# Seven block products in the first half of the gMLP input (z1), and a reordered gating

## The chip, the cores and the metric

One core of a Trainium2 chip runs the whole kernel. The metric is the device time of one execution in microseconds; the median of three runs stands for the kernel. The profile is of one further execution, and gives a start and a duration for every instruction on TensorE (PE, with its weight loads as PEld), VectorE (DVE), ScalarE (ACT), GpSimd (POOL) and for the DMAs issued from SyncE (SP) and ACT.

## The reference

A transformer layer in bf16 with 2048 tokens and a width of 1024: a memory attention block, then a gMLP block. The change touches the second one alone:

```python
def _B_ref(x, w_in, w_sp, b_sp, w_out):
    B, S, D = x.shape                     # S = 2048, D = 1024
    F = w_in.shape[-1]                    # 3584
    Fh = F // 2                           # 1792
    z = _gelu(jnp.einsum('bsd,df->bsf', x, w_in))
    z1 = z[..., :Fh].copy()
    z2 = _layernorm(z[..., Fh:], axis=-1)
    g = jnp.einsum('ts,bsf->btf', w_sp, z2) + b_sp[None, :, None]
    return jnp.einsum('bsf,fd->bsd', z1 * g, w_out)
...
h2 = h + _B_ref(_layernorm(h, axis=-1), B_w_in, B_w_sp, B_b_sp, B_w_out)
```

So there are four large products: the z2 half of the input (2048 x 1024 by 1024 x 1792), the z1 half (the same size), the gating (2048 x 2048 by 2048 x 1792), and the output (2048 x 1792 by 1792 x 1024).

## The kernel before, in words

The program is written with a recorder (`_Recorder`, line 34): each call such as `pe.matmul` or `dve.tensor_tensor` is noted on its engine's list in program order, the waits are worked out from the memory cells and PSUM banks that it reads and writes, and every engine then runs its own list in order. Hence nearly all instructions carry line 210. What sets the order on an engine is the order of the calls; a call that must wait holds everything behind it on its engine, SP's DMA queue included. SBUF is one arena in which tensors are placed by hand (`tens`, with an offset in KB); a new tensor at an old place waits for the last reader of the old one.

After the attention, the gMLP has these stages:

- **z2** (`z2_group`, line 798, and the loop from line 931): 64 groups of 8 matmuls, one for each of 16 token tiles and four chunks of 448 columns. The weights are loaded by `win_load`. ACT takes each bank through a gelu into `Z2`, DVE computes its statistics (`z2_stats`), Pool the reciprocal deviations `ZRS`, and `z2_apply` normalizes a token tile into f16 (`Z2H`). The same loop reads the gating matrix row by row (`sp_norm_load` from SP, into two buffers `SJ`) and sums its squares on ACT (`sp_norm`), from which `sp_scale` makes a power of two `SC` and its inverse `INV`, to keep f16 in range. Eight PSUM banks are used in turn (`next_bank`).
- **z1** (lines 1073 to 1104): four token segments of 512 by 14 feature chunks of 128. Each is 8 matmuls over the width (`mm8`), with a weight chunk of `WIZ` (bf16) against `HNT[s]`, the transposed normalized tokens, and ACT takes the bank through the gelu into `Z1T`. Beside it, DVE does the rest of `z2_apply` and prepares the gating's operands: `sp_load` reads blocks of the gating matrix by transposing DMAs, `sp_half` scales a block to f16, `sp_sum` makes T1, T2, T3 and `s_sum` the sums of Z2 blocks (`SS`).
- **gating** (`gate_group`, line 1001): twice (for tokens 0 to 1023 and for 1024 to 2047) seven groups. A group makes a 2 x 2 block of outputs, 1024 tokens by two feature chunks, with seven block products of 8 matmuls in place of eight (Winograd's form of Strassen's scheme). The seven pair A11, A12, A22 and four sums of the Z2 blocks with B11, B21, B22 and T1 to T4 of the gating matrix. DVE adds products that are shared, with the scale and the bias, and multiplies by `Z1T` in place; ACT copies the first product out, and Pool adds the two bias rows to it.
- **output** (`out_unit`): 16 units of 14 matmuls after each gating half, added to what the attention block left in DRAM. The blocks for the second half of the gating are loaded and prepared beside the first 16 units.

In the gating the order of the products over the engines is written out by hand in `gate_group`: each addition on DVE that reads a bank must be done before TensorE adds the next product to the same bank.

Of the kernel before, what the change touches and what calls it, by code (L numbers as in the profile page):

```python
# [5 lines left out]
BF16 = mybir.dt.bfloat16  # L6
# [252 lines left out]
def bass_sequential_preLN__memory_aug_infini_attn__mixer_gmlp__prompt_kernel(  # L259
# [31 lines left out]
    class Bump:  # L291
# [4 lines left out]
        def __call__(self, name, shape, dt):  # L296
# [63 lines left out]
    WIN = [tens("win%d" % i, [128, 8, 512], BF16, o * K) for i, o in enumerate((46, 54, 190))]  # L360
    WIZ = [tens("wiz%d" % i, [128, 8, w], BF16, o * K)
           for i, (o, w) in enumerate(((54, 512), (190, 512), (118, 512), (126, 256)))]
# [3 lines left out]
    ROLES = (("b11", 46), ("b12", 22), ("b21", 198), ("b22", 14))  # L366
    RAW = {k: tens(k + "r", [128, 8, L], BF16, o * K) for k, o in ROLES}
    BH = {k: tens(k + "h", [128, 8, L], F16, o * K)
          for k, o in ROLES + (("t1", 30), ("t2", 190), ("t3", 22), ("t4", 38))}
    SS = tens("ss", [128, 4, 8, 128], F16, 54 * K)  # L370
# [3 lines left out]
    ZRS = b3("zrs", [128, NTC], F32)  # L374
    ONES = b3("ones", [128, 128], BF16)
    MHZ = b3("mhz", [128, 1], F32)
    SQ = b3("sq", [128, 16], F32)
    SQB = b3("sqb", [128, 16], BF16)
    TOT = b3("tot", [128, 1], F32)
    TOP = b3("top", [128, 1], F32)  # L380
    SC = b3("sc", [128, 1], F32)
    INV = b3("inv", [128, 1], F32)
# [3 lines left out]
    BROW = [tens("brow%d" % i, [128, L], BF16, (132 + i) * K) for i in range(2)]  # L386
    WO0 = tens("w_out0", [128, 14, 512], BF16, 118 * K)
    WO1A = tens("w_out1a", [128, 7, 512], BF16, 54 * K)
    WO1B = tens("w_out1b", [128, 7, 512], BF16, 4 * K)
    FIN = [tens("fin%d" % i, [128, 512], BF16, o * K) for i, o in enumerate((61, 11, 12, 13))]  # L390
# [399 lines left out]
    CH = [("z2", FH + 448 * k, 448) for k in range(4)] + [("z1", 512 * k, min(512, FH - 512 * k)) for k in range(4)]  # L790

    def win_load(k):
        kind, lo, w = CH[k]
        sp.dma_start((WIN[k % 3] if k < 4 else WIZ[k - 4])[:, :, 0:w], wcols(B_w_in, lo, lo + w))

    zs, zq, staged = [], [], []

    def z2_group(k, tc, stage=None):
        s, tcl = divmod(tc, 4)
        b = next_bank()  # L800
        wi = WIN[k % 3]
        mm8(PS[:, b, 0:448], lambda i: HNT[s][:, i, tcl * 128:(tcl + 1) * 128], lambda i: wi[:, i, 0:448])
        if stage is None:
            z2_gelu(k, tc, PS[:, b, 0:448])
        else:
            act.activation(ZSTG[stage][:], PS[:, b, 0:448], ACTF.Copy)
            staged.append((k, tc, ZSTG[stage][:]))
# [5 lines left out]
    def z2_stats():  # L813
        k, tc = zs.pop(0)
        dve.bn_stats(ZST[:, tc, k, :], Z2[:, tc, k * 448:(k + 1) * 448])
        if k == 3:
            dve.bn_aggr(ZMV[:, tc, :], ZST[:, tc, :, :])
            pool.tensor_single_scalar(ZRS[:, tc:tc + 1], ZMV[:, tc, 1:2], float(LN_EPS), ALU.add)
            pool.tensor_tensor(ZRS[:, tc:tc + 1], ZRS[:, tc:tc + 1], MHALF[:], ALU.pow)
            zq.append(tc)  # L820

    def z2_apply():
        tc = zq.pop(0)
        dve.tensor_scalar(Z2H[:, tc, :], Z2[:, tc, :], ZMV[:, tc, 0:1], ZRS[:, tc:tc + 1], ALU.subtract, ALU.mult)

# [93 lines left out]
    def sp_scale(b):  # L919
        pe.matmul(PS[:, b, 0:16], ONES[:], SQB[:], start=True, stop=True)  # L920
        dve.tensor_reduce(out=TOT[:], in_=PS[:, b, 0:16], axis=mybir.AxisListType.X, op=ALU.add)
        dve.tensor_single_scalar(TOT[:], TOT[:], 1e-30, ALU.max)
        pool.tensor_tensor(TOP[:], TOT[:], MHZ[:], ALU.pow)
        dve.tensor_single_scalar(TOP[:].bitcast(I32), TOP[:].bitcast(I32), 0x7F800000, ALU.bitwise_and)
        dve.tensor_single_scalar(SC[:], TOP[:], 8192.0, ALU.mult)
        dve.reciprocal(INV[:], SC[:])

# [3 lines left out]
    for it in todo:  # L931
# [9 lines left out]
        if it[0] and it[1] > 3 or it[0] > 1:  # L941
            q = 16 * it[0] + it[1] - 20
            r = (q * 16 + 15) // 44
            if r < 16 and (q * 16 - 1) // 44 < r:
                sp_norm(r)
                if r < 14:
                    sp_norm_load(r + 2)
                elif r == 15:
                    pool.tensor_copy(SQB[:], SQ[:])
# [4 lines left out]
        if len(zq) > 1:  # L954
            z2_apply()
        if it == (0, NTC - 1):
            win_load(3)
        if it == (1, NTC - 1):
            for k in (4, 6, 7):
                win_load(k)  # L960
        if it == (2, NTC - 1):
            win_load(5)
# [8 lines left out]
    def sp_half(k):  # L971
        dve.tensor_single_scalar(BH[k][:], RAW[k][:], SC[:], ALU.mult)

    def sp_sum(o, a, b):
        dve.tensor_tensor(BH[o][:], BH[a][:], BH[b][:], ALU.subtract)
# [20 lines left out]
    def prod1(g):  # L996
        b = next_bank()
        prod(b, a_blk(0, 0, g), "b11", True)
        return b

    def gate_group(pr, g, ba):
        t1, t2 = slice(1024 * pr, 1024 * pr + 512), slice(1024 * pr + 512, 1024 * pr + 1024)
        s1, s1b1, s1b2, u2, u3 = (TMP[k][:] for k in ("s1", "s1b1", "s1b2", "u2", "u3"))
        inv = INV[:]

        def stt(o, b, add):
            dve.scalar_tensor_tensor(o, bank(b), inv, add, ALU.mult, ALU.add)

        def out(v, i, t):
# [3 lines left out]
        act.activation(s1, bank(ba), ACTF.Copy, scale=inv)  # L1013
        pool.tensor_tensor(s1b2, s1, BROW[1][:], ALU.add)
        pool.tensor_tensor(s1b1, s1, BROW[0][:], ALU.add)
        bb, bc = next_bank(), next_bank()
        prod(bb, SS[:, 1], "t2", True)
        prod(bc, SS[:, 0], "t1", True)
        stt(u2, bb, s1b2)
        if pr == 0 and g == 0:  # L1020
            sp_sum("t4", "b21", "t2")
        if g < 6:
            s_sum(1, g + 1)
        prod(bb, SS[:, 2], "t3", False)
        prod(ba, a_blk(0, 1, g), "b21", False)
        stt(u3, bb, s1b2)
        stt(u3, bc, u3)
        out(u3, 1, t2)
        nb = prod1(g + 1) if g < 6 else None
        if g < 6:  # L1030
            s_sum(3, g + 1)
        stt(s1, ba, BROW[0][:])
        out(s1, 0, t1)
        prod(bc, SS[:, 3], "b22", False)
        if g < 6:
            s_sum(2, g + 1)
        prod(bb, a_blk(1, 1, g), "t4", False)
        stt(u2, bc, u2)
        out(u2, 0, t2)
        if g < 6:  # L1040
            s_sum(4, g + 1)
        stt(s1b1, bb, s1b1)
        out(s1b1, 1, t1)
        return nb
# [24 lines left out]
    for j in range(4):  # L1069
        sp_load(0, "b21", j)  # L1070
    for j in range(4):
        sp_load(0, "b11", j)
    for s in range(NSEG):
        for fc in range(14):
            k, fl = divmod(fc, 4)
            b = next_bank()
            mm8(bank(b), lambda i: WIZ[k][:, i, fl * 128:(fl + 1) * 128], lambda i: HNT[s][:, i, :])
            act.activation(Z1T[:, fc, s * 512:(s + 1) * 512], bank(b), ACTF.Gelu_apprx_tanh)
            if zq:
                z2_apply()  # L1080
            if s == 0 and fc == 6:
                sp_scale(next_bank())
            if s == 2 and fc in (6, 12):
                for k in ("b21", "b11", "b22") if fc == 6 else ("b12",):
                    sp_half(k)
            if s == 3:
                if fc == 0:
                    sp_sum("t1", "b12", "b11")
                if fc == 4:
                    s_sum(1, 0)  # L1090
                    s_sum(2, 0)
                    s_sum(3, 0)
                    s_sum(4, 0)
                if fc == 2:
                    sp_sum("t3", "b22", "b12")
                if fc == 8:
                    sp_sum("t2", "b22", "t1")
        if s == 0:
            for j in range(4):
                sp_load(0, "b22", j)  # L1100
        if s == 1:
# [82 lines left out]
```

## Time and profile before

| | |
|---|---|
| median of 3 runs | 772.08 us (772.01 to 772.38) |
| the profiled execution | 772.03 us |
| its span in the profile | 770.3 us |
| TensorE busy | 761.2 us (99%), 5476 matmuls |
| DVE, ACT, POOL busy | 464.5, 334.2, 200.0 us |
| z2 from its last attention part to z1 | 338.3 to 404.6 us |
| z1 | 404.6 to 501.3 us |
| first gating half, output units, second gating half | 501.3, 586.0, 634.4 us to 719.2 us |
| a matmul of 512 columns, in a row of them | recorded with 379 ns, the next one starts some 216 ns later |

How to read it: the page's span is the time from the first to the last instruction. Matmuls are pipelined, so the duration of one is longer than the distance to the next, and their ends are modelled; the pace is read from a stretch of time and the number of matmuls that were issued in it. (A few per cent of the matmul records can be missing.) In a timeline line the columns are the start, the duration, the engine, the operation with output and inputs, the shapes, the count, and in brackets the idle time before it with what ended it. A group's line ends in its busy time, the mean of one in ns, and the idle time before it.

### The profile page before, as it was taken

What the parts mean: (1) busy time and instruction counts of PE and PEld (TensorE: products, weight loads), DVE (VectorE), ACT (ScalarE), POOL (GpSimd) and SP (SyncE); (2) the same over time, 40 slices, a digit from 0 to 9 for tenths busy, and PEclk for the clock granted to TensorE, in tenths of its full rate; (3) what the DMA queues carried; (4) which work ended last, traced back from release to release, by engine and by line L of the source; (5) the groups of instructions that cost most, each with busy time, mean ns of one, the idle gap of its engine ahead of it and who ended that gap; (6) DMA issues with size and microseconds to landing.
All of it is one profiled execution on the core that took longest, in us unless ns stands there. A gap on an engine that the chain in (4) does not pass through costs nothing.

```text
span 770.3 us, 13128 instructions
## 1 busy us (share of the span) xinstructions
PE 761.2 (99%) x5476; PEld 367.2 (48%) x5551; DVE 464.5 (60%) x846; ACT 334.2 (43%) x395; POOL 200.0 (26%) x361
## 2 busy tenths in 40 slices
PE   8999999999999999999999999999999999999998
PEld 4445555545554545455554444444444444444444
DVE  5586589768964676754366202278785756878422
ACT  6777877777777767157783333310000000000000
POOL 2564556555653333100033000021110002112000
PEclk9999999999999999999999999999999999999999
DMA  9654555364425331765672230020019850000222
GB/s 305 168 152 89 97 83 125 83 97 84 96 57 131 84 83 37 210 173 183 198 219 55 55 67 2 1 96 1 1 34 206 229 169 7 1 1 0 62 83 75
DMA packets 133900, 75.06 MB, mean 97 GB/s; under 512 B 96208, under 2 KB 124624, under 8 KB 133840
## 3 DMA queue, kind: packets, MB, share of 16 engines
q1 hardware_dynamic: 126592, 67.40, 36.0%
q10 hardware_dynamic: 7248, 6.82, 2.8%
q8 instruction: 43, 0.70, 0.4%
q14 instruction: 17, 0.14, 0.1%
HBM read 42.74 MB, written 8.39 MB: 66 GB/s over the span
## 4 chain that ended last, share of the span: by engine, by line
PE 93%; DVE 5%; issue 1%; DMA 1%; ACT 0%; DVEq 0%
PE ps L210 93%; DVE stats L210 1%; DMA wv<-in_A_wv_dram 1%; DVE hch L210 1%; DVE otok L210 0%; DVE pqk L210 0%; DVE lno L210 0%; DVE ta L210 0%; DVE etmp L210 0%; DVE rd L210 0%; DVE rdm L210 0%; DVE mv L210 0%; ACT e L210 0%; ACT L210 0%; DVE upd L210 0%
## 5 line engine op out<-in xcount | busy, mean ns | idle before, releaser
L210 ACT ACTIVATE e<-ps 128x2048 bf16<-128x2048 f32 (+1 forms) x96 | 152.7, 1590 | 41.7 <-PE ps L210 41.5
L210 POOL TENSOR_SCALAR_AFFINE_SELECT e<-e 128x512 bf16<-128x512 bf16 x128 | 90.6, 720 | 132.4 <-ACT e L210 132.3
L210 POOL TENSOR_TENSOR tmp_s1b<-tmp_s,brow 128x512 f32<-128x512 f32 x28 | 32.3, 1155 | 255.1 <-ACT tmp_s L210 223.7
L210 PE MATMUL ps<-win,hnT 128*128 128x448 bf16 x512 | 98.3, 352 | 0.0
L210 PE MATMUL ps<-hnT,wiz 128*128 128x512 bf16 x439 | 96.2, 379 | 0.5
L210 ACT ACTIVATE tmp_s<-ps,inv 128x512 f32<-128x512 f32 x14 | 9.6, 687 | 195.1 <-DVE z1T L210 131.6
L210 PEld LDWEIGHTS ps<-win,hnT 128*128 128x128 bf16 x512 | 49.7, 98 | 46.4 <-issue 0.2
L210 PEld LDWEIGHTS ps<-hnT,wiz 128*128 128x128 bf16 x448 | 43.7, 98 | 52.7
L210 ACT ACTIVATE z1T<-ps 128x512 bf16<-128x512 f32 x56 | 33.4, 597 | 63.3 <-PE ps L210 61.1
L210 PE MATMUL ps<-xnT,wk 128*128 128x512 bf16 x233 | 59.6, 380 | 1.2
L210 PE MATMUL ps<-wv,xnT 128*128 128x512 bf16 x255 | 59.5, 380 | 0.9 <-DMA wv<-in_A_wv_dram 0.5
L210 PE MATMUL ps<-wo,oT 128*128 128x512 bf16 x254 | 57.7, 380 | 0.1
L210 DVE BATCH_NORM_STATS2 zst<-z 128x6 f32<-128x448 bf16 x64 | 38.4, 617 | 31.8 <-ACT z L210 31.3
L210 DVE TENSOR_TENSOR fin<-fin,ps 128x512 bf16<-128x512 bf16 (+2 forms) x33 | 22.1, 671 | 56.6 <-PE ps L210 48.4
L210 PE MATMUL ps<-xnT,wq 128*128 128x512 bf16 x226 | 54.0, 379 | 1.6
L210 PE MATMUL ps<-w_out,z1T 128*128 128x512 bf16 x218 | 49.3, 379 | 0.3
L210 ACT ACTIVATE z<-ps 128x448 bf16<-128x448 f32 x60 | 31.5, 541 | 37.4 <-PE ps L210 37.4
L210 PEld LDWEIGHTS ps<-v,e 128*128 128x128 bf16 x1280 | 38.8, 96 | 14.0 <-issue 6.5
L210 PE MATMUL ps<-v,e 128*128 128x33 bf16 x1280 | 42.2, 178 | 0.0
L210 DVE SCALAR_TENSOR_TENSOR tmp_u<-ps,inv,tmp_s1b 128x512 f32<-128x512 f32 x28 | 21.0, 750 | 31.3 <-PE ps L210 16.7
L210 PEld LDWEIGHTS ps<-wo,oT 128*128 128x128 bf16 x256 | 24.1, 98 | 27.6
L210 PEld LDWEIGHTS ps<-xnT,wk 128*128 128x128 bf16 x256 | 22.6, 98 | 29.9 <-issue 5.0
(137 smaller groups left out, 1101.0 us busy)
## 6 DMA issues: line engine op xcount, KB each, us to landing
sj<-in_B_w_sp_dram SPq DMA_DIRECT2D x16, 512.0 KB, 3.5
xch<-in_A_x_dram SPq DMA_DIRECT2D x16, 256.0 KB, 3.6
xr<-in_A_x_dram SPq DMA_DIRECT2D x16, 256.0 KB, 4.0
out_dram<-hch SPq DMA_DIRECT2D x16, 256.0 KB, 2.4
win<-in_B_w_in_dram SPq DMA_DIRECT2D x4, 896.0 KB, 5.3
wiz<-in_B_w_in_dram SPq DMA_DIRECT2D x3, 1024.0 KB, 6.2
wo<-in_A_wo_dram SPq DMA_DIRECT2D x1, 2048.0 KB, 8.7
fin<-out_dram ACTq DMA_DIRECT2D x16, 128.0 KB, 3.4
```

The source lines that it names most:

```text
L210: ins = getattr(e, op.name)(*op.args, **op.kw)
```

## The change

It has four parts.

1. **z1 by seven block products.** The width is cut into two halves j, the tokens of a pair p of segments into two halves k, and the feature chunks into fc and fc + 7. A group g (14 of them: p = 0 or 1, fc = 0 to 6) makes four output chunks from seven products of 4 matmuls each. They pair four weight blocks and four sums `SZ` of weight blocks (Pool, `sz_sum`) with four token blocks `hb` and four differences `HT` of token blocks (DVE, `hn_sum`; product 5 and 6 use SZ1 and SZ2, 7 uses SZ3, 3 uses SZ4). The weights are now f16 (`WZH`), scaled by a power of two: `wz_norm` takes the largest absolute value of each part, `scale_of` makes scale and inverse, `wz_half` scales. All this happens in the z2 stage, from a list `aux` by step of its loop (step 0 is group (1, 4)). In a z1 group, ACT copies product 1 out of its bank (s1), DVE adds s1 to product 6 (u2) before product 7 is added to the same bank, then u3 = bank + s1 and u3 += product 5, later s1 += bank after product 4 and u2 += bank after product 3; ACT runs the gelu, with the inverse scale, on the four results. The products of all groups are issued in the order of 7 g + `offs`, so that in steady state TensorE does 6, 5, 1 of the next group, 7, 2, 3 of the group before, 4.
2. **What runs beside z1.** No `z2_apply` is left in the z2 stage: 16 of them run in groups 0 to 7, half on DVE, half on ACT (with a small Pool operation before it). The squares of the gating matrix are done by step 35 instead of 41. The scale of the gating is computed in group 1. B11, B12 and B22 are scaled by ACT in quarters (`sp_part`) in groups 8, 9 and 11, B21 by DVE after z1 (`seam`); T1 to T3 are made by DVE in quarters in groups 10 to 13, and T4 in the first gating group (`mid`). Their loads move into z1, B21's to its end.
3. **Gating.** The same seven products, in another order: three first products before the first group, and the second product of group g + 1 within group g; the banks are fixed (0 to 2 for the first product, 3 and 4, 5 and 6 for the others) instead of taken in turn.
4. **Places.** Weights, blocks, `SS`, `BROW`, `FIN` and the output weights lie elsewhere; there is a fourth `WIN` buffer.

The diff, cut to its core:

```diff
+    WZS = ((46, 256), (118, 256), (126, 256), (54, 128))
+    WZ = [tens("wz%d" % i, [128, 8, 2, w], BF16, o * K) for i, (o, w) in enumerate(WZS)]
+    WZH = [tens("wzh%d" % i, [128, 8, 2, w], F16, o * K) for i, (o, w) in enumerate(WZS)]
-    ROLES = (("b11", 46), ("b12", 22), ("b21", 198), ("b22", 14))
+    ROLES = (("b11", 14), ("b12", 22), ("b22", 46), ("b21", 126))
...
+    def scale_of(k, n, b):
+        b = next_bank() if b is None else b
+        pe.matmul(PS[:, b, 0:n], ONES[:], SQB[:, 0:n], start=True, stop=True)
+        dve.tensor_reduce(out=TOT[:], in_=PS[:, b, 0:n], axis=mybir.AxisListType.X, op=ALU.add)
         dve.tensor_single_scalar(TOT[:], TOT[:], 1e-30, ALU.max)
+        if k:
+            dve.reciprocal(TOP[:], TOT[:])
+        else:
+            pool.tensor_tensor(TOP[:], TOT[:], MHZ[:], ALU.pow)
         dve.tensor_single_scalar(TOP[:].bitcast(I32), TOP[:].bitcast(I32), 0x7F800000, ALU.bitwise_and)
+        dve.tensor_single_scalar(SC[k][:], TOP[:], 8192.0, ALU.mult)
+        dve.reciprocal(INV[k][:], SC[k][:])
...
+    def wz_norm(q, r):
+        v = WZ[q][:, 2 * r:2 * r + 2, :, :] if q < 3 else WZ[q][:, 4 * r:4 * r + 4, :, :]
+        dve.tensor_reduce(out=SQZ[:, 4 * q + r:4 * q + r + 1], in_=v.rearrange("p c i w -> p (c i w)"), axis=mybir.AxisListType.X, op=ALU.max,
+                          apply_absolute_value=True)
...
+    def hn_sum(p, t, h, eng=dve):
+        a, b = {1: (hb(0, 1, p), hb(0, 0, p)), 2: (hb(1, 1, p), HT[p][1][:]),
+                3: (hb(1, 1, p), hb(0, 1, p)), 4: (hb(1, 0, p), HT[p][2][:])}[t]
+        s = slice(2 * h, 2 * h + 2)
+        eng.tensor_tensor(HT[p][t][:, s, :], a[:, s, :], b[:, s, :], ALU.subtract)
...
+    def sz_sum(g, k):
+        fc = g % 7
+        a, b, op = {1: (wz_blk(1, 0, fc), wz_blk(1, 1, fc), ALU.add), 2: (sz(g, 1), wz_blk(0, 0, fc), ALU.subtract),
+                    3: (wz_blk(0, 0, fc), wz_blk(1, 0, fc), ALU.subtract),
+                    4: (wz_blk(0, 1, fc), sz(g, 2), ALU.subtract)}[k]
+        pool.tensor_tensor(sz(g, k), a, b, op)
...
+    for r in range(16):
+        q = (37 * r + 15) // 16
+        at(q, sp_norm, r)
+        if r < 14:
+            at(q, sp_norm_load, r + 2)
+    at(37, pool.tensor_copy, SQB[:], SQ[:])
+    for k in range(12):
+        at(k + 1, wz_norm, (1, 2, 0)[k // 4], k % 4)
+    for k in range(8):
+        at(3 + 2 * k, hn_sum, 0, (1, 2, 3, 4)[k // 2], k % 2)
+    at(18, wz_norm, 3, 0)
+    at(19, wz_norm, 3, 1)
+    at(20, pool.tensor_copy, SQB[:, 0:14], SQZ[:])
+    at(25, scale_of, 1, 14, None)
+    for k in range(8):
+        at(26 + k, wz_half, k // 2, k % 2)
+    for k in (1, 2, 3, 4):
+        at(35 + k, sz_sum, 0, k)
...
         if it == (0, NTC - 1):
+            for k in (1, 2, 0):
+                wz_load(k)
             win_load(3)
...
-            mm8(bank(b), lambda i: WIZ[k][:, i, fl * 128:(fl + 1) * 128], lambda i: HNT[s][:, i, :])
-            act.activation(Z1T[:, fc, s * 512:(s + 1) * 512], bank(b), ACTF.Gelu_apprx_tanh)
+        for i in range(4):
+            pe.matmul(b, ka[:, i, :], kb[:, i, :], start=(first and i == 0), stop=(i == 3), skip_group_check=True)
+        if k == 1:
+            act.activation(s1, b, ACTF.Copy)
+        if k == 6:
+            dve.tensor_tensor(u2, b, s1, ALU.add)
+        if k == 5 and g < 13:
+            for x in (1, 2):
+                sz_sum(g + 1, x)
+        if k == 7:
+            dve.tensor_tensor(u3, b, s1, ALU.add)
+            dve.tensor_tensor(u3, bank(zb[g, 2]), u3, ALU.add)
+            z1_out(fc + 7, 2 * p + 1, u3)
+            if g < 13:
+                sz_sum(g + 1, 3)
+        if k == 2:
+            z1_out(fc, 2 * p, b)
+            if g == 0:
+                sz_sum(1, 4)
+        if k == 4:
+            dve.tensor_tensor(s1, b, s1, ALU.add)
+            z1_out(fc + 7, 2 * p, s1)
+        if k == 3:
+            dve.tensor_tensor(u2, b, u2, ALU.add)
+            z1_out(fc, 2 * p + 1, u2)
+            if g < 12:
+                sz_sum(g + 2, 4)
+        for f, a in todo1.get((g, k), ()):
+            f(*a)
...
+    for g in range(8):
+        on(g, 6, lambda: zq and z2_apply())
+        on(g, 4, lambda: zq and z2_apply(True))
+    for k in range(8):
+        on((0, 1, 2, 3, 4, 4, 5, 5)[k], 3 if k < 5 else (7, 3, 7)[k - 5], hn_sum, 1, (1, 2, 3, 4)[k // 2], k % 2)
+    on(1, 7, scale_of, 0, 16, None)
+    for k, g, r in (("b11", 6, 3), ("b12", 6, 3), ("b22", 8, 3), ("b21", 12, 3)):
+        for j in range(4):
+            on(g, r, sp_load, 0, k, j)
+    for n, (k, g) in enumerate((("b11", 8), ("b12", 9), ("b22", 11))):
+        for r in range(4):
+            on(g, (6, 7, 2, 4)[r], sp_part, k, r)
+    for r in range(4):
+        on(10 + r // 2, (3, 6, 3, 6)[r], sp_sum, "t1", r)
+        on(12 + r // 2, (3, 6, 3, 6)[r], sp_sum, "t3", r)
+        on(13, (5, 7, 2, 4)[r], sp_sum, "t2", r)
+    on(7, 3, brow_load, 0)
+
+    offs = {1: -5, 6: 0, 5: 1, 7: 3, 2: 4, 4: 6, 3: 12}
+    for x, g, k in sorted((7 * g + offs[k], g, k) for g in range(14) for k in offs):
+        z1_step(g, k)
```

The gating's new loop (its first lines make products 1 of groups 0 to 2, then `seam`, then product 2 of group 0):

```diff
+        for g in range(7):
+            bb, bc = 3 + g % 2, 5 + g % 2
+            prod(bb, SS[:, 1], "t2", True)
+            prod(bc, SS[:, 0], "t1", True)
+            stt(u2, bb, s1b2)
+            if g == 0:
+                mid()
+            ss(1, g + 1)
+            ss(2, g + 1)
+            if 1 <= g <= 3:
+                p1(g + 2)
+            prod(bb, SS[:, 2], "t3", False)
+            if g < 5:
+                copy1(g + 1)
+                p2(g + 1)
...
+            stt(u3, bb, s1b2)
+            stt(u3, bc, u3)
+            out(u3, g, 1, t2)
...
+            if g != 5:
+                c11(min(g + 1, 6))
+            prod(bb, a_blk(1, 1, g), "t4", False)
+            stt(s1b1, bb, s1b1)
+            out(s1b1, g, 1, t1)
...
+            prod(bc, SS[:, 3], "b22", False)
+            stt(u2, bc, u2)
+            out(u2, g, 0, t2)
+            ss(4, g + 1)
```

## The prediction, made before the changed kernel ran

> **What bounds the kernel now.** I read the page's busy lines and slices first, then the stretches of the z2, z1 and gating stages, then DVE beside Pool in the gating.
>
> ```profile
> span 770.3 us, 13128 instructions
> PE 761.2 (99%) x5476; PEld 367.2 (48%) x5551; DVE 464.5 (60%) x846; ACT 334.2 (43%) x395; POOL 200.0 (26%) x361
> ...
> PE   8999999999999999999999999999999999999998
> ```
>
> ```profile
> 338.30:404.60 66.30, 66.30 (x353) 34.25 (x351) 30.18 (x55) 51.61 (x76) 6.22 (x16) 1.00 0.64 197
> 404.60:501.30 96.70, 96.23 (x442) 43.85 (x450) 27.27 (x39) 33.60 (x57) 7.29 (x18) 1.00 0.19 36
> 501.30:586.00 84.70, 84.70 (x394) 38.31 (x393) 65.93 (x93) 5.41 (x8) 16.14 (x14) 1.00 0.18 42
> ```
>
> The columns are the stretch's length, busy time and instructions of PE, weight load, DVE, ACT and Pool, then clock, DMA share and GB/s. TensorE never rests: z1 is 448 products of 128x128x512 in 96.70 us, 0.2158 us each; one gating half is 392 in 84.70, the same rate. The z1 stretch has much free time on DVE (27 of 97 us), ACT (34) and Pool (7); z2 has little on ACT (52 of 66). So a product taken out of z1 is worth its whole 0.2158 us, as long as the three helpers feed TensorE.
>
> ```profile
> 514.17 1.15 POOL L210 TENSOR_TENSOR tmp_s1b<-tmp_s,brow 128x512 f32<-128x512 f32 x1 [7.71 <-ACT tmp_s L210]
> 514.67 1.20 DVE L210 TENSOR_TENSOR z1T<-tmp_u,z1T 128x512 bf16<-128x512 f32 x1
> ...
> 517.17 0.69 DVE L210 TENSOR_TENSOR z1T<-tmp_s1b,z1T 128x512 bf16<-128x512 f32 x1
> ```
>
> The same DVE form takes 0.69 us alone, but 1.20 when it meets a Pool sum: it ends 0.55 us after Pool does (515.32 to 515.87). Pool's own time stays 1.15 to 1.16.
>
> [...] the trace has 1.156 with f32 in. No f16 sum on Pool is in it. [...] the trace's 128x512 one took 0.685 us, so 1.22 for 1024 is my estimate[...]. [...] In the trace the 512 KB wiz load behind two of 1 MB landed only 11.2 us after its issue[...].
>
> **The change, part by part.**
>
> *TensorE.* z1 becomes 14 groups of 7 products of 4 matmuls: 392 for 448, 56 x 0.2158 = 12.1 us less. Gating keeps 7 x 7 x 8 twice. One more tiny scale product: +0.1. Matmuls with f16 weights and bf16 moving data are new (3 of 7 products); bf16 alone and f16 alone both run at 0.2158, so I take that; the bad end is twice as long for 168 of them, +36.
>
> *Pool in z1.* Four 128x512 sums a group, 4 x 1.156 = 4.6 us, of a period of 28 x 0.2158 = 6.04. The ends for one f16 sum: 0.72 (Pool's one-input affine_select of the same shape) to 2.3 (twice). Value 1.156. SZ1 and SZ2 are released when product 5 of the group before is read and needed five slots later (one slot is 4 matmuls, 0.86 us): 4.3 us for 2.3. So Pool is fed[...].
>
> *DVE in z1.* Five additions a group with one PSUM input, 5 x 0.69 (the ta<-ps row) = 3.5 us; in groups 0 to 7 a z2_apply of 0.74; eight input differences of 0.69 (ss<-z2h row), one a group up to 3, two in 4 and 5; twelve pieces of T1 to T3, 0.69 each, in groups 10 to 13. The extras all meet Pool. What matters is the addition u2: it must read product 6 before product 7 may follow into its bank. Between them lie products 5 and 1 of the next group, 1.73 us. Take from that 0.27 from slot end to DVE start (529.13 to 529.40 in the trace), 0.69, and about 0.25 back (a weight load begins 0.21 before its matmul): 0.5 us of slack. A difference queued ahead of s1 and u2 finds Pool in its fourth sum, ends 0.55 after that, and u2 comes about 0.45 late the first time. A late group starts Pool earlier against DVE, so later ones lose about 0.1.
>
>
> The ledger of a group with one difference, in us from the start of its product 6, if nothing was late: u2 read 1.13 to 1.82; z2_apply to 2.5, ahead of Pool, whose four sums then run 2.3 to 6.9 (the third and fourth wait for products 7 and 3 to be read); u3 twice, 3.7 to 5.1; u2 of the group before, 5.45 to 6.1; the difference, blocked by Pool's fourth sum, ends 6.9 + 0.55 = 7.45 instead of 6.8; s1 to 8.1; next u2 to 8.8; product 7 can start at 9.05, and was due at 6.04 + 2.59 = 8.63. So:
>  - group 1 also computes the gating's scale: DVE waits there for a Pool power queued behind three sums, then does three small steps of 0.17 and a difference: u2 of group 2 is 1.5 late;
>  - single differences: 0.4 in sum; groups 4 and 5 with two each: 0.65 twice, 1.3;
>  - T1 pieces in groups 11 and 12: 0.5, and 1.0 at group 13, where no product 1 lies between 6 and 7.
>
> *ACT in z1.* Per group one copy (0.60) and four gelus (0.69 with a scale operand), 3.4 us; eight z2_apply of 1.7 (between the 0.95 us 1024 and the 1.91 us 2048 rows) up to group 7; twelve operand pieces of about 1.05 in groups 8, 9 and 11. Groups 8 and 9 hold 7.6 us for 6.0; the lag reaches some 4 us and the copy that u2 of group 11 adds is 0.3 late. The operands' transposes come from SP earlier in z1, as regions fall free: b12's after product 3 of group 6; four land about 8.5 us, or ten slots, later, when ACT, in its lag, is just coming to them; b22's land five slots ahead. If b12 came 3 us later, ACT's lag would pass to u2: within the range below. z1 in sum: 1.5 + 0.4 + 1.3 + 1.5 + 0.3 = 5.0 us of stall. The ends: 0, if Pool's sum is 0.9 or less and the slack swallows the rest; 10, at 1.35 a sum[...].
>
> *z2 stage.* SP now issues three wz pairs (3 MB), then win3, at the start, and the third sj load stands behind them. Two 512 KB loads of 512 B rows take 2.0 us each, by the packet times of wiz; sj 1.5; win 3.1: sj2 lands near 354.7, while ACT reaches its square near 348. TensorE runs on: eight banks cover 12 us. But DVE's statistics wait for ACT behind it. DVE needs 14 maxima x 1.22 + 8 x 0.69 + 20 x 0.6 = 34.6 us for 20 groups that last 30.3, and loses some 5 in these waits; by my ledger the last maximum is ready near 379, and TensorE asks for its scale after step 25, at 338.4 + 26 x 1.51 = 377.7. Stall 1.5 us (0 to 5). The scaled weights are done before z1; Pool's first sums too.
>
> *Seam.* b21 is loaded last: its region is free when product 4 of group 12 ends, 7 slots (6.0 us) before z1 does. Four transposes took 5.8 us to issue and about 8.5 until landed; then 1.28 to scale. Needed after three first products of gating, 3 x 1.73: 11.2 for 9.9. Hidden by 1.3, more if z1 stalls; without those three products it would cost 4.
>
> *Gating.* The same DVE work, about 9.8 us a group. Groups without a first product last 6 x 1.73 = 10.4, so it fits; group 0 also makes T4 (4 x 0.61), which holds t4 back by 0.3. Reordered additions end before the output units need them. The moved w_out and second-half loads have some 40 us. Nothing else moves.
>
> *Sum,* against the profiled execution (772.03, its 770.3 span and 1.7 around it, 0.05 below the median 772.08): 772.0 - 12.1 + 0.1 + 5.0 + 1.5 + 0.3 = 766.8.
>
> **The rivals.** *All is hidden* (0.20): [...] Pool's f16 sums took 0.9 or less; 760.0, up to 763. For it: DVE has 0.5 to 2 us a group free. Against: the 1.20 us line. *Pool sets the pace* (0.15), the slower one: [...] past 6.9 us a period, that is 1.5 us a sum, the 0.86 us a group that the products save is gone. At 1.7 a sum: 7.65 a period, 14 x 1.6 = 22 us of stall, 784 with the rest. For it: f16 sums on Pool are unknown; against: 1.156 us is seen with a mixed f32 and bf16 pair. *The load queue starves z2* (0.11): sj behind 4 MB at half the assumed rate empties ACT until the banks run out, 5 us more in z2, 771, and a third of it within 0.2% of before. *Mixed matmuls are slow* (0.04): above 790. That the products aren't saved can't be: 56 fewer are issued.
>
> **How the numbers follow.** The likeliest case, chance 0.50, is 763 to 770, its middle 766.8. All hidden 0.20, starved 0.11 (faster 0.07, same 0.04), Pool pace 0.15, mixed 0.04. About 0.2% (1.5 us) is what a measurement of this kernel can tell from no change. Faster 0.77, same 0.04, slower 0.19. The range 759.8 to 774.5 leaves out most of Pool's pace, mixed, and a sliver below, some 0.18.
>
> **What would show it.** z1's first to last matmul should last 84.6 + 5 us, with PE idle before product 7 put down to DVE (u2), most in groups 2, 5, 6 and 13; DVE's differences at 0.9 to 1.2 us beside 0.69 alone; Pool's sums near 1.16; a PE gap of 1 to 2 us before the first scale product; gating halves at 84.7 to 85.1. Pool sums over 1.5 us, or PE waiting on Pool in every group, would make me wrong upward; PE gaps below 1 us in all z1, downward.

## The result, and the profile after

The changed kernel takes 767.98 us (median of four runs, 766.32 to 769.22), the kernel before 772.23 us: a ratio of 0.9944, with a 95% interval of 0.9924 to 0.9963. It was run again later, with 767.35 us (766.61 to 768.48) against 772.11, ratio 0.9941 (0.9924 to 0.9958). So it is some 4.5 us faster, where 5.3 were forecast. Fifty-six products went, worth 12.1 us; about 7.5 us of stall took their place. The interest lies in where these are, since much of them is not where the prediction put it.

The page's busy lines, answering to the first lines shown of before (761.2 us busy, 99%, DVE 60%, Pool 26%):

```profile
span 767.5 us, 13399 instructions
PE 755.6 (98%) x5496; PEld 360.5 (47%) x5496; DVE 542.9 (71%) x961; ACT 369.9 (48%) x429; POOL 275.0 (36%) x426
```

The profiled execution took 769.22 us. DVE and Pool have 78 and 75 us more to do, and TensorE, at 98%, has begun to wait. The stretches of z2, z1 and the first gating half, with the columns as before:

```profile
339.40:406.10 66.70, 66.70 (x355) 34.53 (x354) 51.58 (x91) 50.89 (x76) 14.09 (x28) 1.00 0.59 179
406.10:495.20 89.10, 85.84 (x395) 37.45 (x393) 71.50 (x106) 68.52 (x88) 72.26 (x72) 1.00 0.28 51
495.20:582.20 87.00, 85.32 (x394) 38.02 (x393) 76.27 (x107) 6.87 (x10) 17.68 (x14) 1.00 0.17 41
```

z2 still runs without a pause: 66.70 of 66.70. z1 is 89.1 us where it was 96.7; its 392 matmuls at 0.2158 us are 84.6, so 4.5 are stall. The gating half, which had none, is 87.0 where it was 84.7. In z1 Pool went from 7 to 72 us busy and DVE from 27 to 72. Whom TensorE waits for is told by the list of its waits (total, number, longest):

```profile
PE ps L210 <- DVE zt L210: 2.7, 4, 0.9
PE ps L210 <- DVE tmp_u L210: 2.4, 5, 0.8
PE ps L210 <- DMA wv<-in_A_wv_dram: 1.7, 1, 1.7
...
PE ps L210 <- POOL sz L210: 0.6, 1, 0.6
```

`zt` is the work space of z1 (s1, u2, u3), `tmp_u` that of the gating, `sz` the sums of weight blocks. The third line is the attention's first wait, for its value weights. It was 0.5 in the profile of before, nothing was changed there, and it goes from none to 1.8 in the profiles below: it can move any one execution by up to 1.8 us. These waits count from the moment at which the engine could have gone on; the gaps in the row of matmuls, counted from where the next one was due, are a little longer. Read from the starts of the matmuls they are, in us:

| where | predicted | first profile | second profile (run again) |
|---|---|---|---|
| z2, at the scale product of the weights | 1.5 | 0 | 0 |
| z1, groups 0 and 1 (not foreseen) | 0 | 1.05 + 0.72 | 0 + 0.25 |
| z1, groups 1 to 2, the gating's scale | 1.5 | 0.18 + 0.92 | 0.18 + 0.92 |
| z1, single differences | 0.4 | 0 | 0 |
| z1, double differences in groups 4 and 5 | 1.3 | 0.43 | 0.44 |
| z1, T1 pieces; ACT's lag | 0.5; 0.3 | 0 | 0 |
| z1, group 13 | 1.0 | 0.94 | 0.95 |
| gating, first group with T4 | 0.3 | 0.23 + 0.93 | 0.23 + 0.93 |
| gating, before `t3`, twice in each half | 0 | 4 x 0.58 | 4 x 0.58 |
| sum | 6.8 | 7.7 | 6.2 |

### The profile page after: what moved, and what is told of

Read it like the earlier page. It is cut to its first block, busy times and chain, and to the rows that moved or that the text cites. A ratio compares the mean times of both kernels' runs of the same rounds, so it can differ in the third digit from the quotient of the medians.

```text
span 767.5 us, 13399 instructions
## 1 busy us (share of the span) xinstructions
PE 755.6 (98%) x5496; PEld 360.5 (47%) x5496; DVE 542.9 (71%) x961; ACT 369.9 (48%) x429; POOL 275.0 (36%) x426
## 4 chain that ended last, share of the span: by engine, by line
PE 80%; DVE 7%; ACT 4%; DMA 3%; issue 2%; POOL 2%; ACTq 0%; POOLq 0%; DVEq 0%
PE ps L210 80%; ACT sj L210 3%; DMA sj<-in_B_w_sp_dram 2%; DVE tmp_u L210 2%; DVE ss L210 1%; DVE zt L210 1%; POOL sz L210 1%; DMA wv<-in_A_wv_dram 1%; POOL zrs L210 1%; ACT z L210 1%; DVE z1T L210 1%; DVE tmp_s1b L210 0%; DVE t4h L210 0%; DVE t2h L210 0%; DVE ht L210 0%
## 5 line engine op out<-in xcount | busy, mean ns | idle before, releaser
L210 POOL TENSOR_SCALAR_AFFINE_SELECT e<-e 128x512 bf16<-128x512 bf16 x128 | 90.7, 722 | 132.1 <-ACT e L210 132.0
L210 POOL TENSOR_TENSOR tmp_s1b<-tmp_s,brow 128x512 f32<-128x512 f32 x28 | 34.0, 1219 | 184.0 <-ACT tmp_s L210 82.7
L210 PE MATMUL ps<-w_out,z1T 128*128 128x512 bf16 x336 | 74.0, 379 | 0.0
L210 PE MATMUL ps<-xnT,wq 128*128 128x512 bf16 x256 | 60.5, 379 | 0.0
L210 DVE TENSOR_TENSOR zt<-ps,zt 128x512 f32<-128x512 f32 x70 | 47.4, 686 | 14.8 <-PE ps L210 12.2
L210 PEld LDWEIGHTS ps<-w_out,z1T 128*128 128x128 bf16 x336 | 32.9, 98 | 39.6
L210 DVE RECIPROCAL rd<-ps 128x16 f32<-128x16 f32 x32 | 8.0, 250 | 47.0 <-PE ps L210 46.8
L210 ACT ACTIVATE z1T<-zt,inv 128x512 bf16<-128x512 f32 x42 | 29.7, 718 | 17.3 <-DVE zt L210 17.2
L210 DVE TENSOR_TENSOR z1T<-tmp_u,z1T 128x512 bf16<-128x512 f32 x42 | 35.8, 853 | 1.4
```

Source lines behind the costliest of these rows:

```text
L210: ins = getattr(e, op.name)(*op.args, **op.kw)
```

## The experiments

Unless said otherwise a kernel is the changed one with the edit shown; ratios are to the kernel before, beside it on the same chip.

### The new gating order alone

The kernel before, with the changed kernel's `gate` in place of the two loops over `gate_group`; T4 is made by `sp_sum` as it was before.

```diff
-    nb = prod1(0)
-    for g in range(7):
-        nb = gate_group(0, g, nb)
+    gate(0, mid=lambda: sp_sum("t4", "b21", "t2"))
```

> The kernel before with only the new order of the gating (z1 and its operands as before). Theory: the new gating itself costs time, because from the end of one group's T3 product to the start of the next one's DVE has a chain of eleven steps, about 9.4 us with its two meetings with Pool's bias sums, and groups of six products leave only 8.6 us; two gaps of 0.6 us in each half, and about 0.9 us where T4 is made in the first group: 775.4, gating halves of 86.8 and 85.9 us. Rival: the gaps come from the late B21 and the other things that z1 leaves to the gating; then this kernel is at 772.2 with both halves at 84.7.

Measured: 774.5 us (773.72 to 776.83), ratio 1.0029 (1.0019 to 1.0039): slower by some 2 us. The gaps in its gating are 0.59, 0.59, 0.58 and 0.58, all before the product with `t3` in groups without a first product: 2.3. So part 3 of the change costs time by itself, whatever z1 does. The 0.9 us that the expectation put on T4 did not come: here DVE makes T4 in one step of 2.28 us, has nothing left over from z1, and `t4` follows without a pause. For that one gap of the changed kernel, 0.93, the rival fits.

### z1 alone, with the old gating order

The changed kernel with the old loops, `prod1` and `gate_group`; B21 and T4 are prepared in the first group, and no first products run ahead.

```diff
-    gate(0, seam, mid)
+    nb = prod1(0)
+    for k in range(1, 5):
+        s_sum(k, 0)
+    for g in range(7):
+        nb = gate_group(0, g, nb)
```

> The changed kernel with the gating in the old order (old banks in turn, one first product ahead); the Z2 sums of the first group are made right after z1, B21 is scaled in the first gating group. Theory: the 3.5 us of gaps in the two gating halves go, about 0.8 come at the seam because the first two sums are only begun when z1 ends: 765.3, second gating half 84.7. Rival (gaps caused by what z1 leaves behind): the second half is the same as in the changed kernel and the time 767 to 769.

Measured: 768.66 us (767.26 to 768.84), ratio 0.9946 (0.9932 to 0.9961): the expectation missed by 3.4, and the time lies where the rival had it. But the rival's reason fails: the second half of the gating has no gap, as the theory said. What the theory missed is in the first half, which opens with gaps of 2.62, 0.32, 0.59 and 0.95. The timeline of the seam shows why: DVE makes the last pieces of T2 and T3 among the last additions of z1, then the sums of Z2, and TensorE stands for these.

```profile
493.66 1.89 PE L210 MATMUL ps<-b11h,z2h 128*128 128x512 f16 x8
...
495.94 0.68 DVE L210 TENSOR_TENSOR t3h<-b22h,b12h 128x1024 f16<-128x1024 f16 x1
...
496.54 0.68 DVE L210 TENSOR_TENSOR ss<-z2h 128x1024 f16<-128x1024 f16 x1
...
497.87 1.64 DVE L210 TENSOR_TENSOR ss<-z2h 128x1024 f16<-128x1024 f16 x1
498.01 1.25 PE L210 MATMUL ps<-t2h,ss 128*128 128x512 f16 x5 [2.46 <-DVE ss L210]
```

One product (`b11h`) is all that TensorE has between z1 and the sums. The three first products ahead of the changed gating, 3 x 1.73 us, cover this. By the gaps, then, the new order costs 3.5 us and saves 4.5. That it pays is read from the gaps alone: the times of the two kernels, with ratios of 0.9946 and 0.9944, are too close to show it.

### The weight sums of group 0, earlier in z2

```diff
-        at(35 + k, sz_sum, 0, k)
+        at(27 + k, sz_sum, 0, k)
```

> The changed kernel with Pool's four weight sums of group 0 eight steps earlier in the z2 stage (steps 28 to 31 instead of 36 to 39). Theory: the first two gaps in z1 (1.05 and 0.72 us) come from Pool, which serves these sums among the deviations of the last token tiles and so falls behind, and DVE, whose next statistics wait for Pool's reads, with it; moved early, the backlog is gone at z1's start: both gaps vanish, 766.2, z1 87.4. Rival: DVE is late by its own work (maxima, statistics, scaling), then the gap of 1.05 stays.

Measured: 766.39 us (765.8 to 766.64), ratio 0.992 (0.9905 to 0.9935). Both gaps at the start of z1 are gone. In the changed kernel's first profile these four Pool sums stand among the reciprocal deviations of the last token tiles; DVE's statistics, which wait for these, stood 1.2 us for Pool three times in a row and came to the first addition of z1 late:

```profile
401.78 0.26 DVE L210 BATCH_NORM_AGGREGATE zmv<-zst 128x2 f32<-128x24 f32 x1 [1.21 <-POOL zrs L210]
```

In the second profile the same sums ran 1.8 us earlier against z1's start, and only 0.25 was lost. So this one profile doesn't show that the edit took the gaps away, and the profiles of all kernels with the new z1 have to be laid side by side. The three in which the last of the four sums began some 2 us before z1 lost 1.8 us at its start. The six in which it began 3.4 to 4.0 us before lost between none and 0.5, with the sums where they were; two of them, z1 alone and the reordered gating, lost nothing. The two with the sums moved began it 13 us before and lost nothing. The loss goes with the lateness of the sums, and the edit gives them much room; what makes them late in some executions was not settled.

### The gating's scale, finished a group later

```diff
-    on(1, 7, scale_of, 0, 16, None)
+    on(1, 7, scale_of, 0, 16, None, False)
+    on(2, 7, scale_tail, 0)
```

`scale_tail` is the end of `scale_of`, from the `bitwise_and` on: all that reads Pool's power. What it moves is seen in the timeline of the changed kernel:

```profile
419.19 1.15 POOL L210 TENSOR_TENSOR sz<-wzh 128x512 f16<-128x512 f16 x1
...
419.29 0.15 DVE L210 TENSOR_SCALAR tot<-tot 128x1 f32<-128x1 f32 x1
...
420.30 0.55 POOL L210 TENSOR_TENSOR top<-tot,mhz 128x1 f32<-128x1 f32 x1
...
420.88 0.16 DVE L210 TENSOR_SCALAR top<-top 128x1 int32<-128x1 int32 x1 [1.45 <-POOL top L210]
...
423.87 0.60 PE L210 MATMUL ps<-z1x,sz 128*128 128x512 f16 x2 [0.76 <-DVE zt L210]
```

The power (0.55 us) stands behind a sum of 1.15, DVE stands for 1.45, and the addition that TensorE needs ends 0.76 late.

> The changed kernel with the gating's scale in two parts: sum and Pool's power in group 1 as before, the three small DVE steps that need the power only in group 2. Theory: the gap of 0.92 us before product 7 of group 2 comes from DVE standing at the power, which Pool reaches after three sums; without the stand it goes: about 0.9 us less than the changed kernel, 767.1. Rival: the difference queued behind it and its meeting with Pool's fourth sum make the gap; then at least half of it stays.

Measured: 766.7 us (765.31 to 767.26), ratio 0.9922 (0.9907 to 0.9937). The two gaps at group 2 are gone; that of the double differences stays (0.36), and so does group 13's (0.95). This settles the term of the scale: 1.1 us by the gaps, for the 1.5 predicted.

### The gating's additions, reordered

```diff
             stt(u2, bb, s1b2)
             if g == 0:
                 mid()
-            ss(1, g + 1)
-            ss(2, g + 1)
+            else:
+                s_sum(4, g)
+                ss(1, g + 1)
+                ss(2, g + 1)
...
             stt(u3, bc, u3)
+            if g == 0:
+                ss(1, 1)
+                ss(2, 1)
             out(u3, g, 1, t2)
...
             out(u2, g, 0, t2)
-            ss(4, g + 1)
```

> The changed kernel with two moves on DVE in the gating: the fourth Z2 sum of the next group comes after that group's first addition u2, and in the first group the first two sums come after the two u3 additions instead of before them. Theory: the chain from T3's end to the next T3 gets 0.6 us shorter and the four gaps of 0.58 us go; T4's gap of 0.93 goes too: halves of 84.7 to 85.0, 3.2 us less than the changed kernel, 764.8. Rival: DVE is full in groups of six products, so the step only moves the wait; then gaps of 0.4 or more stay in both halves.

Measured: 763.58 us (763.06 to 765.18), ratio 0.9888 (0.9873 to 0.9903). Its first gating half lasts 85.14 us for the changed kernel's 86.98, its second 84.86 for 85.79. That is 2.8 us; the median is 4.4 us lower, but this kernel's profile also has no loss at the start of z1 (1.77 in the changed kernel's first) and a wait for the value weights of 0.3 for 1.7, which the edit doesn't touch. First the changed kernel, from one `t3` to the next, in the timeline:

```profile
545.05 0.75 DVE L210 SCALAR_TENSOR_TENSOR tmp_u<-ps,inv,tmp_s1b 128x512 f32<-128x512 f32 x1 [1.81 <-PE ps L210]
...
545.88 1.16 POOL L210 TENSOR_TENSOR tmp_s1b<-tmp_s,brow 128x512 f32<-128x512 f32 x1 [5.78 <-DVE tmp_u L210]
...
546.62 0.96 DVE L210 TENSOR_TENSOR z1T<-tmp_u,z1T 128x512 bf16<-128x512 f32 x1
...
551.66 1.09 DVE L210 TENSOR_TENSOR z1T<-tmp_u,z1T 128x512 bf16<-128x512 f32 x1
551.76 1.89 PE L210 MATMUL ps<-t1h,ss 128*128 128x512 f16 x8
...
552.68 0.68 DVE L210 TENSOR_TENSOR ss<-z2h,ss 128x1024 f16<-128x1024 f16 x1
553.28 0.74 DVE L210 SCALAR_TENSOR_TENSOR tmp_u<-ps,inv,tmp_s1b 128x512 f32<-128x512 f32 x1
553.94 0.68 DVE L210 TENSOR_TENSOR ss<-z2h 128x1024 f16<-128x1024 f16 x1
554.08 1.90 PE L210 MATMUL ps<-t3h,ss 128*128 128x512 f16 x8 [0.43 <-DVE tmp_u L210]
```

At 545.05 the addition u3 reads the bank that `t3` has just left; the next `t3` is due five products after the last one, 5 x 1.73 = 8.63 us, at 553.50. But u2 (553.28), which frees its bank, stands behind all the group's additions and outputs on DVE. Two of these meet Pool (0.96 and 1.09 for 0.69), and one, `ss<-z2h,ss`, has no hurry. u2 ends at 554.02, and TensorE is 0.58 late. With the edit:

```profile
547.75 1.89 PE L210 MATMUL ps<-t1h,ss 128*128 128x512 f16 x8
...
548.77 0.75 DVE L210 SCALAR_TENSOR_TENSOR tmp_u<-ps,inv,tmp_s1b 128x512 f32<-128x512 f32 x1
549.44 0.68 DVE L210 TENSOR_TENSOR ss<-z2h,ss 128x1024 f16<-128x1024 f16 x1
549.58 1.90 PE L210 MATMUL ps<-t3h,ss 128*128 128x512 f16 x8
```

The sum stands behind u2, and `t3` starts 1.83 us after `t1h`, 0.1 late where it was 0.58.

### A fifth sum on Pool, to ask how near its pace is

```diff
             if g < 13:
                 sz_sum(g + 1, 3)
+                sz_sum(g + 1, 3)
```

> The changed kernel with SZ3 formed twice in each group, so that Pool does five sums instead of four. Theory: Pool has 6.04 - 4 x 1.16 - 0.25 = 1.1 us a group free[...], so a fifth sum fills the period in groups 0 to 7 and gaps follow: z1 longer by 4 to 8 us, 772 to 776. Rival: Pool's slack and the lead of the sums swallow it, only DVE's own queue sets the gaps: within 1 us of 768.

Measured: 773.94 us (771.73 to 775.86), ratio 1.0019 (1.0012 to 1.0027), slower than before and within the theory's interval: z1 lasts 94.3 us for 89.1, and one more sum of 1.2 us a group undoes the gain. But much of it seemed lost at one place. DVE waited 4.02 us there for the power of the scale, TensorE stood 2.27 and 0.92, and then its granted clock fell, as two stretches of the trace show:

```profile
423.90:427.40 3.50, 3.50 (x10) 1.23 (x9) 1.71 (x3) 2.75 (x4) 3.33 (x3) 0.51 0.00 0
427.70:431.20 3.50, 3.50 (x18) 1.61 (x17) 3.09 (x5) 1.75 (x4) 2.29 (x4) 1.00 0.01 2
```

In the first the clock is 0.51 and the matmuls start every 0.427 us; ten of them cost 1.9. That makes 5.1 us that could belong to the scale's place alone, 1.1 of which the changed kernel loses there too. So the same was tried with the scale finished a group later, as above:

> SZ3 is formed twice, as in the kernel with a fifth sum, but the gating's scale is finished a group later, so that VectorE doesn't stand waiting for Pool's power. Theory: of the 6 us that the fifth sum cost, 5.1 arose at that one place (TensorE idle 2.27 and 0.92, and then ten matmuls at half pace, 1.9), and Pool, though busy 5 x 1.2 = 6.0 of 6.04 us a group, holds nothing else up but the two groups with double differences: 769 us. Rival (Pool's occupation sets the pace of every group): over 772.

Measured: 773.23 us (771.59 to 775.94), ratio 1.0017 (1.001 to 1.0024). The theory fell and its rival held: nothing was won. The clock stays at 1.00, the wait at the scale is gone, and the time is lost in small parts, group by group. In its list of waits, the line that had 0.6 in the changed kernel's is on top:

```profile
PE ps L210 <- POOL sz L210: 5.2, 9, 1.0
```

One group in its timeline, from one wait to the next:

```profile
439.38 2.84 POOL L210 TENSOR_TENSOR sz<-wzh 128x512 f16<-128x512 f16 x2
439.48 1.90 PE L210 MATMUL ps<-z1x,sz 128*128 128x512 f16 x8 [0.72 <-POOL sz L210]
...
441.17 1.54 DVE L210 TENSOR_SCALAR z2h<-z,zmv,zrs 128x1792 f16<-128x1792 bf16 x1
...
442.18 1.53 POOL L210 TENSOR_TENSOR sz<-wzh,sz 128x512 f16<-128x512 f16 x1
...
443.69 0.27 POOL L210 TENSOR_SCALAR znm<-zmv,zrs 128x1 f32<-128x1 f32 x1
443.92 1.16 POOL L210 TENSOR_TENSOR sz<-wzh 128x512 f16<-128x512 f16 x1
...
445.15 1.49 POOL L210 TENSOR_TENSOR sz<-sz,wzh 128x512 f16<-128x512 f16 x1
...
446.69 0.60 PE L210 MATMUL ps<-z1x,sz 128*128 128x512 f16 x2 [0.71 <-POOL sz L210]
```

Pool hardly rests, and its work lasts 7.21 us (439.48 to 446.69), which is now TensorE's period too, for the 6.04 that the matmuls need. Five sums alone would be 5.8; the rest is the bias of the next `z2_apply` (0.27) and sums that last longer beside DVE's steps (1.49 and 1.53). In this group a sum that begins while DVE is at a step that reads SBUF alone takes 1.53 in place of 1.15 (442.18), and such a DVE step that begins while a sum runs takes 1.54 in place of 0.73 (441.17).

### Two memsets on Pool

```diff
             if g < 13:
+                for _ in range(2):
+                    pool.memset(sz(g + 1, 3), 0.0)
                 sz_sum(g + 1, 3)
```

This occupies Pool, by 0.52 us each, with work that reads nothing. It asks whether the cost comes from the meetings, in which Pool and DVE read at the same time (769 to 771), or from Pool's being busy.

> The changed kernel with two Pool memsets of SZ3's place in each group ahead of its sum, about as long as the fifth sum of the earlier run (two of some 0.5 us), but they only write. [...] DVE's two-input steps don't grow longer beside them and the loss against the changed kernel is 1 to 3 us (Pool's own lateness): 769 to 771. If only Pool's occupation counts, it loses what the fifth sum lost, 773.9.

Measured: 771.83 us (769.33 to 773.82), ratio 0.9993 (0.9983 to 1.0002). This decides nothing, since the wait at the scale grew here as well (TensorE stood 2.21 and 0.92 us, with six matmuls at about half pace after it; the expectation below has 1.08 for the second stop). So it too was run again with the scale finished a group later:

> Two memsets of SZ3 on Pool ahead of its sum, which read nothing, and the gating's scale finished a group later. Theory: 4.5 of the cost of the memsets arose at the scale (2.21 and 1.08 idle, 1.2 of half pace): 771.8 - 4.5 = 767.3 us, within 1 of the changed kernel. Rival (the time that Pool is busy delays each group): 770 to 772.

Measured: 769.56 us (768.64 to 770.68), ratio 0.9966 (0.9955 to 0.9977): the theory's 767.3 missed, and 0.4 short of the rival's interval. Against the kernel whose scale alone is finished later, z1 is 90.7 us for 87.9, with the same gaps at its start in both. What came in between 418 and 473 us are seven waits for Pool, 0.32 to 0.84 each, and one of 0.24 for DVE, 3.8 in sum, while other gaps fell by 0.9. Yet the DVE step that meets the memsets in its timeline is no longer for it:

```profile
481.96 1.11 POOL L210 MEMSET sz<- 128x512 f16 x2
...
482.45 0.68 DVE L210 TENSOR_TENSOR t1h<-b12h,b11h 128x1024 f16<-128x1024 f16 x1
```

The DVE step runs beside the two memsets and takes 0.68 us, as it does alone; beside one of Pool's sums the same step took 1.39 and 1.47 in the changed kernel's first profile (at 482.21 and 488.27). The five other DVE steps of two inputs that meet nothing but memsets, in this kernel and in the one with the scale in its old place, take 0.68 as well. So here Pool's plain occupation costs the time, the 2.8 us by which z1 is longer. The fifth sum occupies Pool about as long as the two memsets, 1.16 us for 1.11, but it reads, and on the same chip its kernel took 773.23 us, 3.7 more. The longer occupation can make some 0.6 of that (13 times 0.05, an estimate); the rest goes with reading, on top of the occupation. Where TensorE waits for Pool in two groups running, the period is 6.75 us (438.58 to 445.33). Less 1.17 for the memsets, Pool's own work in such a group is about 5.6 of the 6.04 us; that is an estimate, and leaves the changed kernel some 0.4 us a group.

### All mended

The early sums, the later end of the scale and the reordered gating together. Further, the first of the p = 1 differences is made at steps 40 and 42 of z2, the other six halves one a group, and product 2 of group 13 comes before its product 7.

```diff
-    for k in range(8):
-        on((0, 1, 2, 3, 4, 4, 5, 5)[k], 3 if k < 5 else (7, 3, 7)[k - 5], hn_sum, 1, (1, 2, 3, 4)[k // 2], k % 2)
+    for k in range(6):
+        on(k, 3, hn_sum, 1, (2, 3, 4)[k // 2], k % 2)
...
+    for k in (0, 1):
+        at(40 + 2 * k, hn_sum, 1, 1, k)
...
-    for x, g, k in sorted((7 * g + offs[k], g, k) for g in range(14) for k in offs):
+    for x, g, k in sorted((7 * g + offs[k] - 2 * ((g, k) == (13, 2)), g, k) for g in range(14) for k in offs):
```

> The changed kernel with all of it: weight sums of group 0 early, scale split, gating reordered, the two halves of the first input difference of the second pair made in the z2 stage so that no group has two, and product 2 of the last group before its product 7. Theory: each gap is its own mechanism, so the sums add: 1.77 + 0.92 + 3.2 + 0.43 + 0.94 = 7.3 us less than the changed kernel's 768.0, 760.7; z1 at 84.6 to 85.2. Rival: a gap removed lets the next queue run late (DVE has only some 15 us free in z1), so half comes back: 763 to 765.

Measured: 762.1 us (761.79 to 762.64), ratio 0.9866 (0.9851 to 0.9881), the fastest of all. The head of its list of waits:

```profile
PE ps L210 <- DMA wv<-in_A_wv_dram: 1.4, 1, 1.4
PE ps L210 <- DVE etmp L210: 1.2, 1, 1.2
PE ps L210 <- DVE zt L210: 0.5, 1, 0.5
```

The second line belongs to the attention and stands in before's list too, with 1.2. Of the gaps in the table two are left, 0.67 in group 13 and 0.40 in the first gating group. The median lies 1.4 us above the expectation. With four of 0.1 before `t3` these gaps come to 1.5 us, where the expectation left 0.4 of the table's sum; that names 1.1 of the 1.4. The wait for the value weights doesn't: it was 1.7 in the first profile of the changed kernel, from which the expectation starts.

### The changed kernel again

> The changed kernel itself, unaltered, beside the two kernels below on the same chip: 767 to 769 us. The first wait of TensorE, for the attention's value weights, has varied between 0.2 and 1.8 us from run to run and should explain most of its spread.

Measured: 767.35 us (766.61 to 768.48); its profile is the last column of the table, with a span of 764.9 for the first one's 767.5. The first wait for the value weights was 0.8 for 1.7, and z1's start lost 1.5 less: 2.4 of the 2.6 us between the two.

## Why the prediction was right, and which of its steps were not

**TensorE.** The 56 products are worth their 0.2158 us each: z1 is 84.6 us plus its gaps. f16 weights with bf16 data run at the same pace, 0.216 us in the products 1, 2 and 3, so mixed matmuls were no rival. (In each group three weight blocks and three token blocks enter as they are, not four as the section on the change has it; the fourth ones enter in sums and differences alone.)

**Pool's sums.** Taken at 1.156 us from an f32 row; f16 sums measure 1.156 at the median of all 56, and 1.22 on average in z1, with those that a DVE step made longer. The rival in which all is hidden asked for 0.9 or less, and DVE's differences beside Pool took 0.68 to 1.43 us. The slower rival, Pool's pace, was the nearer one: a sum more per group and the gain is gone, by the waits on Pool that it named. The estimate of Pool's load, 4 x 1.156 + 0.85 = 5.5 us a group, stands against about 5.6 found. In the 0.85, on which the 6.9 and 7.65 of that rival rest too, 0.25 is for the bias and 0.6 was my estimate of what meetings with DVE's steps add to Pool's, which no line of before showed; in z1 the four sums are 0.26 longer a group, and the bias takes 0.64 on average, 0.27 at the shortest.

**z1: mechanism right, size too large.** 5.0 was forecast; 2.5 lies at the places that were named. The scale (1.5, measured 1.1) and group 13 (1.0, measured 0.94) nearly held. The additions that read a bank held their 0.69 among Pool's sums (0.63 to 0.69, all 70). Mis-sized were the steps that meet Pool: differences 0.4 + 1.3 (measured 0.44), T1 pieces 0.5 and ACT's lag 0.3 (both 0). The ledger let every difference meet Pool's last sum at its worst moment. In the trace some come as a sum ends (0.68 to 0.87 us), and of the two groups with doubled differences only one was late. That Pool's sums lengthen the differences is read from the times at which they meet; no run takes the sums away from them. The fifth sum against the memsets shows for Pool's work what reading adds.

**z2: the step failed.** ACT's stop was there: 7.36 us of waiting for the third row of the gating matrix, which it could read at 356.7 where 354.7 was forecast. But the 1.5 us at the scale product did not come. The cast ahead of it runs at 376.58 and the product at 378.90, without a gap: DVE had the last maximum some 2.4 us sooner than my ledger, and TensorE asked 1.2 us later:

```profile
378.90 0.17 PE L210 MATMUL ps<-sqb,ones 128*128 128x14 bf16 x1
```

DVE stood 2.45 us for ACT's gelu behind that stop, where "some 5" were put on such waits. A maximum took 1.20 us. The 1.22 was an estimate; the profile of before leads to it as well (a tensor_reduce of 512 columns is the 0.685 of the prediction, and 512 columns more are 0.53 at 1.04 ns, by the `fin` rows of 687 ns for 512 and 286 for 128). What did come was at the start of z1. "Pool's first sums too" were called done in time, and they were, but in three of the nine profiles with the sums in that place they delayed the deviations among which they stand enough to cost 1.8 us; the two with earlier sums lose nothing.

**Seam: the result held, its reason did not.** No gap came at the seam. But B21 was not what was close: its last transpose landed at 493.62, and DVE came to scale it only at 498.20, without a pause before, so DVE's own queue set that time. "Without those three products it would cost 4" was reckoned from B21's load. The kernel with the old order did lose 4.5, but to Z2 sums and late additions on DVE; B21 had landed there at 491.65, 2 us before z1 ended. That the two numbers are near each other is luck.

**Gating: the step that failed most.** It said "The same DVE work, about 9.8 us a group. Groups without a first product last 6 x 1.73 = 10.4, so it fits", and put 0.3 on all of it; the gaps are 3.5, and the halves are 87.0 and 85.8 where 84.7 to 85.1 were to be seen. The total does fit: DVE even rests 0.67 us in such a group. But the rest lies just before `t3` ends, and the work from there to the addition that the next `t3` needs is 9.0 us and a start of 0.2, for 8.63 allowed. A total was compared with a period where a chain should have been compared with the distance between its two ends. The T4 term, 1.2 for 0.3, left out what the seam leaves on DVE: in the changed kernel the first addition u2 begins 1.17 us after `t1h` does, with the new gating order alone 0.20, and there T4 costs nothing. The reordered kernel leaves the total as it was, moves one sum past that addition in each group, and two in the first group past u3; 0.1 is left before `t3`, and nothing at T4.

**The sum.** 6.8 of stall forecast, 7.7 and 6.2 found. Too much was put on z1's named places and on z2 (4.0 in all), too little on the gating (3.2) and the start of z1 (0.25 to 1.8): the forecast owes its nearness to errors of opposite signs.

## What to carry to other kernels

When a product is saved and TensorE must be fed by helpers, check for each bank the chain from the moment that releases it to the addition that is needed next, against the matmuls between the two; a total that fits says nothing. In such a chain put work that nobody waits for behind the addition that TensorE needs, and don't let DVE stand for a small Pool step that is queued behind long ones: here these two moves were worth about 3 us and 1 us by the gaps. And test how near a helper is to the pace by giving it a known piece of work more; one step of 1.2 us a group showed a limit of which the changed kernel's waits tell little.

## What the runs showed of the hardware that was not expected

- A stop can cost more than itself. In two kernels TensorE stood some 2.2 us and, four matmuls later, 0.92 more; of the matmuls after that ten and six started 0.427 us apart, for 0.216 otherwise. With the fifth sum, the granted clock was 0.51 over the 3.5 us shown above. The two stops sum to 3.1 or 3.2 us, with four matmuls between them; a single one of 2.6 at the seam had no such sequel: the five matmuls after it ran at full pace (1.25 us). What decides was not tried.
- An f16 sum of two inputs on Pool is no faster than an f32 one: 1.156 us at the median in both cases, for 512 elements a partition. A memset of the same shape takes 0.52 and, unlike a sum, doesn't slow a DVE step of two inputs: 0.68 us in all six meetings.
- The meetings cost both engines: Pool's sums took up to 1.60 us in z1. That one began at 439.08, while a difference on DVE was running (438.41 to 439.67), which took 1.26 for 0.68 and had itself begun while Pool was at the sum before. That "Pool's own time stays 1.15 to 1.16" was true of the lines before, not of the changed kernel.
